# Attention and feed-forward in one kernel: maxima of keys and means of values of the third and fourth batch follow a table of steps

## The chip, the core and the metric

The kernel runs on one core of one Trainium2 chip. The core has five engines with an instruction queue each: TensorE (PE; its weight loads are shown apart as PEld), VectorE (DVE), ScalarE (ACT), GpSimd (POOL) and SyncE (SP), which here only issues transfers. Every queue is worked off in order, and an instruction that waits for a semaphore holds up all that stand behind it. Sixteen transfer engines move data between DRAM and the on-chip memory SBUF; matmul results stand in PSUM, which has eight banks. The metric is the device time of one execution in microseconds (us), lower is better.

## What is computed

Attention with a window and with summaries of blocks, and behind it a feed-forward layer, all in float32:

```python
# q, k, v: 4 batches, 8 heads, 768 positions, 64 wide; block, window = 32, 16
k_sum = k.reshape(B, H, nb, block, D).max(axis=3)
v_sum = v.reshape(B, H, nb, block, D).mean(axis=3)
scores_l = scale * np.matmul(q, k.transpose(0, 1, 3, 2))      # only where |i - j| < 16
scores_s = scale * np.einsum('bhsd,bhnd->bhsn', q, k_sum) + np.log(block)
a = softmax(concatenate([scores_l, scores_s]))
attn = a @ concatenate([v, v_sum])
x = attn as 3072 tokens x 512
h = x @ w_in                                                   # 512 x 2048
out = (h * tanh(softplus(h))) @ w_out                          # 2048 x 512
```

For each of the 24 blocks of 32 positions the attention needs the maximum of the keys, k_sum, and the mean of the values, v_sum.

## The kernel before

**Tiling.** Two heads make a pair `hp` (four pairs) and 256 positions a chunk `c` (three to a batch, twelve in all). A unit is one pair of one chunk; `todo` lists the 48 units, chunk by chunk. The fourth batch is chunks 9 to 11, units 36 to 47. The feed-forward layer works on six groups `g` of 512 tokens, in 16 columns `fc` of 128 of its 2048 middle values: 96 steps in all. A step is: products with w_in (`ph`), the activation on ScalarE, its split into a rounded part `ah` and a rest `al`, and the products with w_out (`po`) for the column two steps back. All matmuls take operands as a rounded part and a rest, three products for one.

**Stages.** Up to step 18 an order that is written out by hand places every operation. Steps 19 to 31 (about 162 to 245 us) run in a loop in which VectorE also makes sums of weight blocks (`first_sums`, `second_sums`), which go out to DRAM (`w_sums`, line 691) from a work area, the tile `results`; VectorE can write the area again only when the stores have landed. From step 32 on, two steps run together (`ff_in_pair`), with seven products of such sums and of sums of blocks of x (`x_blocks`) in place of eight. Their weights come back from DRAM in turns, 1.8 MB for each pair of steps (`load_sums`, line 725). In this part VectorE also combines the product tiles into `h` (lines 750 to 758), which frees their PSUM banks. The sums of weights end at step 40.

**Attention in the loop.** Two units start at each of the steps 19, 22, 25, 29, 33, 37, and so on by fours (`begins`): scores `sc` there, the transposes `pt_ps` two steps later, the value products `x_ps` at the next begin. Then ScalarE copies x_ps into `x_blocks`, and VectorE makes the operands of the feed-forward products from it (lines 459 to 465).

**Summaries of the blocks.** For each pair of heads of a batch a chain of four operations runs once: `load_key_source` (line 238) loads the keys `ks`, `key_summary` (line 276) takes their maxima into `km` on VectorE, `load_value_source` (line 242) loads the values `vsum`, `value_means` (lines 297 and 298) sums and scales them into `vq` on VectorE. `ks` and `vsum` of all pairs share one buffer, so each load waits until the operation before it in the chain is done. `value_summary` (line 303) then copies vq into the tile `vm`, from which `att_load_values` (line 324) fills the operand of x_ps; GpSimd copies km into the operand of the scores (`att_key_summary`, line 312). The four vm tiles of one batch are written again by the next one.

**What sets the order of these.** In `loads(i)`, called once in each step, the tables `keys` and `sums` say when `att_load_keys` (the maximum and behind it the load of values of one pair) and `att_summaries` (the means, the copy to vm and the load of keys of the next pair) run. For the third batch, with pairs 0 to 3, the maximum stands at steps 23, 25, 27 and 29 and the means one step later; for the fourth at 46, 48, 50, 52 and one step later.

Of the kernel before, what the change touches and what calls it, by code (L numbers as in the profile page):

```python
# [9 lines left out]
F32 = mybir.dt.float32  # L10
# [7 lines left out]
B, H, S, D = 4, 8, 768, 64  # L18
DM, DFF = 512, 2048
BLK, WIN = 32, 16  # L20
P = 128
NB = S // BLK
# [3 lines left out]
CH = 256  # L26
# [3 lines left out]
HP = H // 2  # L30
# [9 lines left out]
TG = CG * CH  # L40
# [29 lines left out]
def fused_kernel(ctx: ExitStack, tc: tile.TileContext, q0, qk, kt, v0, vw, vs, w_in, w_out, out):  # L70
# [3 lines left out]
    def pool(name, bufs, side):  # L74
        return ctx.enter_context(tc.tile_pool(name=name, bufs=bufs, side=side))
# [3 lines left out]
    att = pool("att", 2, "left")  # L79
    w_in_home = pool("w_in_home", 1, "left")  # L80
    maxima = pool("maxima", HP, "left")
# [142 lines left out]
        nc.gpsimd.memset(zeroed[hp][0:KW], 0.0)  # L224

    summary = {}
    xs = {}
    units = {}
    rests = {}
# [42 lines left out]
    def key_summary(b, hp):  # L272

        keys = sources.pop((b, hp, 0))
        km = maxima.tile([P, NB], F32, tag="km", name=f"km{b}_{hp}")
        nc.vector.reduce_max(km, keys.rearrange("p (n j) -> p n j", j=BLK), axis=AX.X)  # L276
        summary[b, hp] = [km]

# [35 lines left out]
    def att_load_keys(c, hp):  # L314
        b, th = divmod(c, CPB)
        if th == 0:
            key_summary(b, hp)
            load_value_source(b, hp)

    def att_load_values(c, hp):  # L320
        b = c // CPB
        vwt = att.tile([KA, NQ, P], F32, tag="vw", name=f"vw{c}_{hp}")
        nc.sync.dma_start(vwt[0:KW], vw[c, hp].rearrange("p (s k) -> p s k", s=NQ))
        nc.sync.dma_start(vwt[KW:KA], summary[b, hp][1].unsqueeze(1).broadcast_to([NB, NQ, P]))
        units[c, hp]["v"] = vwt

    def att_summaries(u):

        for i, fs in ((u, (value_means, value_summary)), (u + 1, (load_key_source,))):
            if i < len(todo) and todo[i][0] % CPB == 0:  # L330
                for f in fs:
                    f(todo[i][0] // CPB, todo[i][1])
# [325 lines left out]
    for k, word in enumerate(order):  # L658
        name, what = parse(word)
# [7 lines left out]
    dram = ctx.enter_context(tc.tile_pool(name="dram", bufs=1, space=bass.MemoryType.DRAM))  # L667
    kept = [dram.tile([P, 2, 7, CH], F32, name=f"w_sums_{p}") for p in range(NFC // 2)]
    whole_steps = WHOLE * NFC
    change = att.tile([P, CH], F32, tag="pt", name="change", bufs=1)  # L670
    area = res[0]

    def home(p):
# [87 lines left out]
    at = {}  # L761

    def put(what, i, *found):
        at.setdefault((what, i), []).extend(found)
# [4 lines left out]
    for k, i in enumerate(begins):  # L769
        pair = [2 * n + 2 + 2 * k, 2 * n + 3 + 2 * k]  # L770
        later = begins[k + 1] if k + 1 < len(begins) else i + 4
        put("scores", i, *pair)
        put("turns", i + 2, *pair)
        put("values", later, *pair)
        for j, u in enumerate(pair):
            put("norms", i + j, u)
            put("copies", i + 1 + j, u + 2)
            shift = {25: 1, 19: -1}.get(i, 0)
            put("keys", i + 1 + 2 * j + shift, u + 4)
            put("sums", i + 2 + 2 * j + shift, u + 4)  # L780

    def found(what, i):
        return [todo[u] for u in at.get((what, i), ()) if u < len(todo)]

    def loads(i):
        for u in at.get(("scores", i), ()):
            if u + 2 < len(todo):
                att_queries(*todo[u + 2])
        for unit_ in found("keys", i):
            att_load_keys(*unit_)  # L790
        for unit_ in found("copies", i):
            att_key_summary(*unit_)
        for u in at.get(("sums", i), ()):
            att_summaries(u)
        for u in at.get(("values", i), ()):
            if u + 2 < len(todo):
                att_load_values(*todo[u + 2])

    def norms(i):
        for unit_ in found("norms", i):  # L800
# [137 lines left out]
```

## Time and profile before

| | us |
|---|---|
| median of 3 runs | 651.85 |
| lowest and highest | 651.17 and 658.01 |
| the profiled execution | 656.05 |
| its span | 654.3 |
| PE busy | 610.8 (93%) |
| DVE busy | 439.7 (67%) |
| ACT busy | 339.6 (52%) |
| POOL busy | 79.6 (12%) |
| mean granted TensorE clock | 0.975 |

The profile is of one execution, and the times in it count from the start of its span. A row of the timeline gives the start and the length of an instruction, or of several alike in a row, and in brackets how long its engine stood idle before it and what released it. Matmuls are pipelined, so consecutive ones overlap. The granted clock is a share of 2.4 GHz; its lower level, 1.2 GHz, is 0.5. "DMA w_sums<-results" as a releaser means that a store to w_sums landed.

### The profile page before, as it was taken

Reading aid. Unit: us, or ns where it says so; the run is one execution under the profiler, and the core shown is the slowest. Engines: PE = TensorE matmul, PEld = TensorE weight load, DVE = VectorE, ACT = ScalarE, POOL = GpSimd, SP = SyncE. Lnnn points to the kernel's source line nnn. Section 1 sums busy time; section 2 is a strip of 40 time slices with the busy share of each in tenths; the row PEclk is TensorE's granted clock in tenths of the full one; section 3 lists DMA queues with packets and bytes.
Section 4 is the critical chain, followed back from the end, with each engine's and each line's share of the span. In section 5 each row is a group of like instructions: output and inputs, shape, how many; then the busy total and the mean of one; then the engine's idle time right before and its main releaser. Section 6 shows DMA issues by size and latency. Waiting matters only on the chain.

```text
span 654.3 us, 13016 instructions
## 1 busy us (share of the span) xinstructions
PE 610.8 (93%) x4848; PEld 527.8 (81%) x4848; DVE 439.7 (67%) x1102; ACT 339.6 (52%) x803; POOL 79.6 (12%) x119
## 2 busy tenths in 40 slices
PE   3899999999999996999499887999999999999997
PEld 3788777788888875898398776988988989898996
DVE  3999999982678585676677664664774665743433
ACT  3887668583556242753255452565566473323322
POOL 4431122110110000101011010110110110000000
PEclk9899999999999997999699988999999999999999
DMA  9978666642577865978678476776586563556411
GB/s 265 244 252 284 216 217 210 200 158 94 166 239 244 286 225 171 328 280 266 224 254 283 156 265 224 251 251 230 193 285 248 172 224 143 195 208 225 143 83 66
DMA packets 50223, 141.78 MB, mean 217 GB/s; under 512 B 8816, under 2 KB 15728, under 8 KB 50160
## 3 DMA queue, kind: packets, MB, share of 16 engines
q1 hardware_dynamic: 50160, 140.94, 64.6%
q8 instruction: 39, 0.64, 0.4%
q14 instruction: 24, 0.20, 0.1%
HBM read 117.83 MB, written 20.97 MB: 212 GB/s over the span
## 4 chain that ended last, share of the span: by engine, by line
PE 50%; DVE 20%; DMA 11%; ACT 4%; issue 3%; SPq 0%; DVEq 0%
PE po L531 24%; PE ph L740 17%; DMA w_sums<-results 6%; PE ph L503 5%; DMA vsum<-vs 4%; PE x_ps L431 2%; DVE al L521 2%; PE sc L347 1%; ACT pr L379 1%; PE pt_ps L405 1%; DVE results L699 1%; DVE vq L297 1%; DVE w L176 1%; DVE km L276 1%; DVE results L707 1%
## 5 line engine op out<-in xcount | busy, mean ns | idle before, releaser
L399 POOL TENSOR_TENSOR pr<-pr,rs 128x480 f32<-128x480 f32 x48 | 57.7, 1204 | 418.5 <-DVE rs L395 252.0
L740 PE MATMUL ph<-xh,w_early_in 128*128 128x256 f32 x512 | 99.2, 278 | 0.0
L531 PE MATMUL po<-w_early_out_hi,ah 128*128 128x512 f32 x240 | 96.2, 401 | 2.5 <-DVE results L541 2.5
L510 ACT ACTIVATE h<-h 128x512 f32<-128x512 f32 x64 | 36.9, 623 | 114.4 <-DVE h L757 114.4
L531 PE MATMUL po<-w_early_out_hi,al 128*128 128x512 f32 x240 | 94.9, 396 | 0.9 <-DVE al L521 0.9
L531 PE MATMUL po<-w_early_out_lo,ah 128*128 128x512 f32 x240 | 94.6, 394 | 0.0
L379 ACT ACTIVATE pr<-pr,nm 128x120 f32<-128x120 f32 x192 | 73.4, 384 | 24.1 <-DVE nm L368 23.9
L740 PEld LDWEIGHTS ph<-xh,w_early_in 128*128 128x128 f32 x512 | 83.4, 191 | 0.0
L521 DVE TENSOR_TENSOR al<-h,ah 128x512 fp32r<-128x512 f32 x64 | 43.1, 691 | 58.1 <-ACT ah L519 58.1
L740 PE MATMUL ph<-xl,w_early_in 128*128 128x256 f32 x256 | 71.3, 278 | 0.0
L531 PE MATMUL po<-w_late_out_hi,ah 128*128 128x512 f32 x144 | 57.1, 397 | 0.0
L531 PEld LDWEIGHTS po<-w_early_out_hi,ah 128*128 128x128 f32 x240 | 46.1, 192 | 13.1 <-DVE results L541 2.9
L531 PE MATMUL po<-w_late_out_hi,al 128*128 128x512 f32 x144 | 56.0, 389 | 0.6 <-DVE al L521 0.6
L531 PE MATMUL po<-w_late_out_lo,ah 128*128 128x512 f32 x144 | 55.9, 388 | 0.0
L531 PEld LDWEIGHTS po<-w_early_out_hi,al 128*128 128x128 f32 x240 | 45.9, 191 | 10.3 <-DVE al L521 2.0
L531 PEld LDWEIGHTS po<-w_early_out_lo,ah 128*128 128x128 f32 x240 | 45.9, 191 | 9.6
L503 PE MATMUL ph<-xh,w_early_in 128*128 128x512 f32 x160 | 52.0, 391 | 0.0
L740 PEld LDWEIGHTS ph<-xl,w_early_in 128*128 128x128 f32 x256 | 48.9, 191 | 0.0
L750 DVE TENSOR_TENSOR change<-h,ph 128x256 f32<-128x256 f32 x32 | 13.1, 410 | 50.5 <-ACT h L749 50.5
L740 PE MATMUL ph<-w_early_in 128*128 128x256 f32 x272 | 41.5, 290 | 3.3 <-DVE w_early_in L464 2.7
L740 PE MATMUL ph<-w_late_in,w_early_in 128*128 128x256 f32 x304 | 43.0, 277 | 0.5 <-DVE w_late_in L465 0.5
L746 ACT COPY h<-ph 128x512 f32<-128x512 f32 x32 | 18.8, 587 | 44.6 <-PE ph L740 44.6
(110 smaller groups left out, 1228.4 us busy)
## 6 DMA issues: line engine op xcount, KB each, us to landing
w_early_in<-w_sums SPq DMA_DIRECT2D x64, 896.0 KB
qk<-qk SPq DMA_DIRECT2D x40, 496.0 KB
w<-w_in SPq DMA_DIRECT2D x16, 512.0 KB
w<-w_out SPq DMA_DIRECT2D x16, 512.0 KB
w_sums<-results SPq DMA_DIRECT2D x32, 256.0 KB
vw<-vw SPq DMA_DIRECT2D x40, 192.0 KB
ks<-kt SPq DMA_DIRECT2D x16, 384.0 KB
out<-results SPq DMA_DIRECT2D x24, 256.0 KB
```

The source lines that it names most:

```text
L176: nc.vector.scalar_tensor_tensor(out=x, in0=high, scalar=SIGN, in1=x, op0=ALU.bitwise_and, op1=ALU.bitwise_or)
L276: nc.vector.reduce_max(km, keys.rearrange("p (n j) -> p n j", j=BLK), axis=AX.X)
L379: nc.scalar.activation(pr[:, s, :], pr[:, s, :], AF.Exp, scale=-1.0, bias=nm[:, s:s + 1], accum_out=sm[:, s:s + 1])
L399: nc.gpsimd.tensor_mul(u["p"], u["p"], u["r"].unsqueeze(2).broadcast_to([P, NQ, KA]))
L431: nc.tensor.matmul(x, u["v"][0:rows, s, d], pt, start=(c >= CG), stop=(c >= CG or s == NQ - 1))
L503: nc.tensor.matmul(turned(ph), w[:, cc * P:(cc + 1) * P], turned(x[:, cc, :]), start=(cc == 0 and n == 0), stop=(cc == NCC - 1 and n == 2))
L510: nc.scalar.activation(a, st[g, fc], AF.Mish)
L521: return lambda: nc.vector.tensor_sub(al, a, ah.bitcast(F32))
L531: nc.tensor.matmul(turned(po[g][t]), a[:, tok], turned(w), start=(fc == 0 and n == 0), stop=(fc == NFC - 1 and n == 2))
L740: nc.tensor.matmul(turned(ps[:, half * CH:(half + 1) * CH]), w_[:, a * P:(a + 1) * P], turned(x[:, a, :]), start=(a == 0 and n == 0), stop ...
L746: nc.scalar.copy(second, products(1, 3))
L750: nc.vector.tensor_sub(change, second[:, high], ps[:, low])
```

## The change

The tables `keys` and `sums` go. A new table, `chain`, gives the step of each operation by batch: it starts at step 19 for the third batch with one step from link to link, and at step 33 for the fourth with two; the value of `sent` is the step of the copy to vm. Within a pair of heads the load of keys stands at some step, the maximum and the load of values one link later, the means one link after that, together with the load of keys of the next pair. So the maxima of the third batch stand at steps 20, 22, 24 and 26, its means at 21, 23, 25 and 27; the maxima of the fourth at 35, 39, 43 and 47, its means at 37, 41, 45 and 49. Since the maxima of the fourth batch are now written while those of the third are still read, they get a place of their own, the second half of a tile (`spare`) whose first half is `change`, a work tile of VectorE.

```diff
-        km = maxima.tile([P, NB], F32, tag="km", name=f"km{b}_{hp}")
+        if b == B - 1:
+            km = maxima_home[0][:, hp * NB:(hp + 1) * NB]
+        else:
+            km = maxima.tile([P, NB], F32, tag="km", name=f"km{b}_{hp}")
...
-    change = att.tile([P, CH], F32, tag="pt", name="change", bufs=1)
+    spare = att.tile([P, TG], F32, tag="pt", name="spare", bufs=1)
+    change = spare[:, :CH]
+    maxima_home.append(spare[:, CH:])
...
-            shift = {25: 1, 19: -1}.get(i, 0)
-            put("keys", i + 1 + 2 * j + shift, u + 4)
-            put("sums", i + 2 + 2 * j + shift, u + 4)
...
+    for b, i, gap, sent in ((2, 19, 1, (22, 24, 26, 28)), (3, 33, 2, (45, 45, 49, 50))):
+        for hp in range(HP):
+            for k, f in enumerate((load_key_source, key_summary, load_value_source, value_means)):
+                chain.setdefault(i + gap * (2 * hp + (k + 1) // 2), []).append((f, b, hp))
+            chain.setdefault(sent[hp], []).append((value_summary, b, hp))
+
+    def in_order(event):
+        return (value_summary, key_summary, load_value_source, value_means, load_key_source).index(event[0])
...
-        for unit_ in found("keys", i):
-            att_load_keys(*unit_)
...
-        for u in at.get(("sums", i), ()):
-            att_summaries(u)
...
+        for f, b, hp in sorted(chain.get(i, ()), key=in_order):
+            f(b, hp)
```

Three places show what moves. In the rows, a number after a name tells the pair of heads or the column; line numbers of the change are 4 to 6 higher than those before for the same operation.

VectorE at steps 30 to 32, before (rs is the divisor of a unit, x_blocks to w_early_in make an operand, al is the rest of an activation):

```order
L394 TENSOR_SCALAR rs_1_2799<-sm_1_2734 128x4
L395 RECIPROCAL rs_1_2799<-rs_1_2799 128x4
L297 TENSOR_REDUCE vq_3_2804<-vsum_3_2754 96x32
L298 TENSOR_SCALAR vq_3_2804<-vq_3_2804 96x32
L464 CAST xh_126<-x_blocks 128x512
L465 TENSOR_TENSOR xl_127<-x_blocks,xh_126 128x512
L459 SCALAR_TENSOR_TENSOR x_blocks<-x_blocks 128x512
L464 CAST w_early_in<-x_blocks 128x512
```

The same place of the change:

```order
L398 TENSOR_SCALAR rs_1_2804<-sm_1_2743 128x4
L399 RECIPROCAL rs_1_2804<-rs_1_2804 128x4
L468 CAST xh_126<-x_blocks 128x512
L469 TENSOR_TENSOR xl_127<-x_blocks,xh_126 128x512
L463 SCALAR_TENSOR_TENSOR x_blocks<-x_blocks 128x512
```

The means of the last pair of the third batch have left the place between the divisor and the operand; they stand three steps earlier.

SyncE at steps 37 to 40, before (w_early_in<-w_sums are weight sums that come back, w_sums<- are their stores):

```order
L324 DMA vw_1_3325<-vm_1_2532 24x4x128
L725 DMA w_early_in<-w_sums_1969 128x1792 x2
L691 DMA w_sums_1970<-w_late_in 128x512 x2
L691 DMA w_sums_1970<-results 128x512 x4
L691 DMA w_sums_1970<-results 128x256 x2
L725 DMA w_early_in<-w_sums_1970 128x1792 x2
L691 DMA w_sums_1971<-w_late_in 128x512 x2
```

The same place of the change:

```order
L328 DMA vw_1_3330<-vm_1_2361 24x4x128
L239 DMA ks_1_3336<-kt 128x768
L731 DMA w_early_in<-w_sums_1969 128x1792 x2
L697 DMA w_sums_1970<-w_late_in 128x512 x2
L697 DMA w_sums_1970<-results 128x512 x4
L697 DMA w_sums_1970<-results 128x256 x2
L243 DMA vsum_1_3464<-vs 96x1024
L731 DMA w_early_in<-w_sums_1970 128x1792 x2
L697 DMA w_sums_1971<-w_late_in 128x512 x2
```

A load of keys and a load of values of the fourth batch have come in, one ahead of the weight sums and their stores, one behind the stores.

VectorE at steps 46 and 47 (pair 48 of steps follows with the sums h), before:

```order
L465 TENSOR_TENSOR w_late_in<-x_blocks,w_late_in 128x512
L276 TENSOR_REDUCE km_0_4023<-ks_0_3918 128x24
L521 TENSOR_TENSOR al_15_4041<-h_15_3945,ah_15_4040 128x512
L297 TENSOR_REDUCE vq_0_4045<-vsum_0_4025 96x32
L298 TENSOR_SCALAR vq_0_4045<-vq_0_4045 96x32
L750 TENSOR_TENSOR change<-h_1_4078,ph_0_1_4093 128x256
```

The same place of the change:

```order
L469 TENSOR_TENSOR w_late_in<-x_blocks,w_late_in 128x512
L525 TENSOR_TENSOR al_15_4065<-h_15_3973,ah_15_4064 128x512
L280 TENSOR_REDUCE spare<-ks_3_3952 128x24
L756 TENSOR_TENSOR spare<-h_1_4098,ph_0_1_4113 128x256
L757 TENSOR_TENSOR spare<-h_1_4098,spare 128x256
```

Where the first pair of heads had its maximum and its means, one directly after the other, the last pair has its maximum now.

## Rows read from the trace of the kernel before

**Rows 1.** By stretch: length, busy PE, PEld, DVE, ACT, POOL, clock, DMA share, GB/s.

```profile
203.00:228.00 25.00, 25.00 (x178) 20.70 (x176) 17.49 (x46) 12.23 (x30) 2.39 (x4) 1.00 0.85 271
...
240.60:263.20 22.60, 15.27 (x77) 13.02 (x75) 14.70 (x33) 9.40 (x24) 2.50 (x4) 0.85 0.64 206
...
263.00:311.00 48.00, 48.00 (x414) 42.95 (x414) 33.48 (x90) 25.79 (x64) 5.44 (x8) 1.00 0.86 291
...
370.00:430.00 60.00, 52.30 (x410) 45.44 (x408) 36.93 (x101) 28.58 (x71) 5.17 (x8) 0.91 0.70 237
```

**Rows 2.** Chain that ended last, pieces of x_ps: start us, us, what.

```profile
263.25 1.08 PE x_ps L431 x32
...
346.17 1.11 PE x_ps L431 x32
...
430.30 1.08 PE x_ps L431 x32
...
453.87 1.11 PE x_ps L431 x32
...
478.10 1.08 PE x_ps L431 x32
```

**Rows 3.** Timeline of VectorE and TensorE, late stretch: start, length, instruction, [idle before].

```profile
382.85 1.22 DVE L297 TENSOR_REDUCE vq<-vsum 96x32 f32<-96x1024 f32 x1 [2.62 <-DMA vsum<-vs]
...
385.99 0.60 PE L531 MATMUL po<-w_early_out_hi,ah 128*128 128x512 f32 x1 [2.52 <-DVE results L541]
...
401.82 1.22 DVE L297 TENSOR_REDUCE vq<-vsum 96x32 f32<-96x1024 f32 x1 [7.83 <-DMA vsum<-vs]
...
404.75 0.63 PE L347 MATMUL sc<-qk 64*64 64x120 f32 x2 [3.35 <-DVE h L752]
```

**Rows 4.** Timeline of SyncE and VectorE, late stretch: loads of vsum, a use.

```profile
366.31 0.34 SPq L242 DMA_DIRECT2D vsum<-vs  x1
...
369.51 1.22 DVE L297 TENSOR_REDUCE vq<-vsum 96x32 f32<-96x1024 f32 x1 [2.63 <-DMA vsum<-vs]
...
393.42 0.33 SPq L242 DMA_DIRECT2D vsum<-vs  x1
```

**Rows 5.** Timeline of VectorE and TensorE, early stretch.

```profile
231.24 1.23 DVE L707 TENSOR_TENSOR results<-w_early_in 128x1024 f32<-128x1024 f32 x1 [8.43 <-DMA w_sums<-results]
...
241.74 0.92 DVE L276 TENSOR_REDUCE km<-ks 128x24 f32<-128x768 f32 x1
...
248.62 0.65 PE L405 MATMUL pt_ps<-ident,pr 128*120 128x128 f32 x4 [3.81 <-POOL pr L399]
...
252.59 1.22 DVE L297 TENSOR_REDUCE vq<-vsum 96x32 f32<-96x1024 f32 x1 [5.19 <-DMA vsum<-vs]
...
256.29 0.35 PE L740 MATMUL ph<-w_early_in 128*128 128x256 f32 x1 [2.66 <-DVE w_early_in L464]
```

**Rows 6.** Timeline of VectorE and TensorE, between the two stretches.

```profile
310.33 0.69 DVE L713 TENSOR_TENSOR results<-results 128x512 f32<-128x512 f32 x1 [4.80 <-DMA w_sums<-results]
...
320.12 0.63 PE L347 MATMUL sc<-qk 64*64 64x120 f32 x2 [8.10 <-DMA w_early_in<-w_sums]
...
325.65 0.69 DVE L713 TENSOR_TENSOR results<-results 128x512 f32<-128x512 f32 x1 [1.98 <-DMA w_sums<-results]
...
329.89 0.96 PE L740 MATMUL ph<-w_early_in 128*128 128x256 f32 x6 [0.32 <-DVE nm L368]
```

**Rows 7.** Timeline of VectorE, GpSimd and TensorE, steps 22 to 27.

```profile
185.49 0.28 DVE L368 CUSTOM_DVE_ANT_0 pr<-sc,base 128x120 f32<-128x120 f32 x1 [1.31 <-PE sc L347]
...
215.94 0.99 POOL L399 TENSOR_TENSOR pr<-pr,rs 128x480 f32<-128x480 f32 x1 [5.85 <-PE ph L503]
...
218.44 1.04 PE L405 MATMUL pt_ps<-ident,pr 128*120 128x128 f32 x8
```

**Rows 8.** Transfers by line: queue, operation, count, KB each.

```profile
vsum<-vs SPq DMA_DIRECT2D x12, 384.0 KB
```

**Rows 9.** Waits of SyncE's queue: what waited, for what, us, times, longest.

```profile
SPq L242 <- DVE km L276: 11.4, 4, 8.6
```

More of the change, by code (lines that the diff above doesn't have):

```diff
@@ L226, in fused_kernel @@
     summary = {}
+    maxima_home = []
     xs = {}
@@ L777, in fused_kernel @@
             put("copies", i + 1 + j, u + 2)
-            shift = {25: 1, 19: -1}.get(i, 0)
-            put("keys", i + 1 + 2 * j + shift, u + 4)
-            put("sums", i + 2 + 2 * j + shift, u + 4)
     def found(what, i):
         return [todo[u] for u in at.get((what, i), ()) if u < len(todo)]
+    chain = {}
+    for b, i, gap, sent in ((2, 19, 1, (22, 24, 26, 28)), (3, 33, 2, (45, 45, 49, 50))):
[5 more added lines that the diff above has]
+        return (value_summary, key_summary, load_value_source, value_means, load_key_source).index(event[0])
     def loads(i):
```

## The prediction

> **What bounds the kernel now.** I read the busy times first: TensorE works in 93% of the span, so what can be won is where it stands still or runs at a low clock. The views by stretch name two such places that hold the moved work [rows 1]: from 240.6 to 263.2 us TensorE is busy 15.27 of 22.60 us at a mean granted clock of 0.85, and from 370 to 430 us 52.30 of 60.00 us at 0.91. Then the chain of work that ended last, whose x_ps pieces (the value product of two units, line 431) mark equal portions of work [rows 2]. In undisturbed work two of them are 453.87 - 430.30 = 23.57 us apart. From 346.17 to 430.30 lie three such portions, in 84.13 us instead of 70.7: 13.4 us are lost there. From 263.25 to 346.17 lie three too, in 82.92 us: 12.2 us lost.
>
> **What ends each loss.** In the late stretch it is the wait for values that were loaded just before their use [rows 3]: VectorE stands at the sum of vsum (line 297) for 2.62 us before 382.85 and 7.83 us before 401.82. Behind it in VectorE's order wait the copies of results and the sums h, which free PSUM banks, and TensorE waits for those, 2.52 us before 385.99 and 3.35 us before 404.75. The reason stands in SyncE's own order: the load issued at 393.42 was used at 401.82, 8.4 us later, the one issued at 366.31 at 369.51, 3.2 us [rows 4]; VectorE ran out of other work in between.
>
> In the early stretch two things add up [rows 5]. VectorE waited 8.43 us, until 231.24, for stores of weight sums to land, and ran late from there. It reached the maximum of keys at 241.74 (0.92 us), while TensorE stood 3.81 us before 248.62 for a normalized unit. Then it waited 5.19 us for vsum and summed it at 252.59 (1.22 us), and only then made the block that TensorE waited for, 2.66 us before 256.29.
>
> Between them lies a third loss that the change doesn't name [rows 6]. VectorE waits until 310.33 and 325.65 (4.80 and 1.98 us) for stores of weight sums, the sums h come late, and TensorE stands 8.10 us before 320.12 and 0.32 us before 329.89. The transfer engines are busy 0.86 of the 48 us before 311, at 291 GB/s [rows 1].
>
> **The change, part by part.** The same 8 maxima, 8 means and 16 loads remain, plus a place for four tiles of maxima; TensorE's and ScalarE's orders don't change. So nothing is removed but waits, and each moved instruction must find room where it goes.
>
> *Fourth batch, late stretch.* The eight waits with load and use in one or two steps become two full steps, about 11.8 us (half of 23.57), against 3.2 to 8.4 us from issue to use above. The three sums and maxima left there (at steps 45, 47, 49) have their data. I take 13.4 us less the 0.7 us that a portion with copies of results loses anyway (478.10 - 453.87 = 24.23 against 23.57 [rows 2]): **-12.7 us**. Bounds: 13.4 if nothing remains, 5.9 if only the two waits shown on TensorE go (2.52 + 3.35) and nothing of the clock comes back.
>
> *Third batch, early stretch.* The maximum at 241.74 goes: 0.92 us less of the 3.81. The wait of 5.19 and the sum of 1.22 go: the 2.66 us vanish, because the block is then ready 6.4 us sooner. The clock: 0.85 on average over 22.60 us is 2 x 0.15 x 22.6 = 6.8 us at the lower of its two levels (1.2 against 2.4 GHz), after waits, which costs up to 3.4 us; half of it, 1.7, belongs to the second wait. Together **-5.3 us**. The wait of 8.43 stays: those stores lie behind the same loads of weight sums in both orders. Bounds: 0.9 (only the maximum counts) and all 7.33 us of idle time with 3.4 of clock, 10.7.
>
> *Third batch, where it goes (steps 19 to 27, about 160 to 220 us).* TensorE doesn't wait there now: it is busy 25.00 of the 25.00 us from 203 [rows 1]. VectorE has gaps (1.31 us before 185.49), and the last slack is at 218.44, where transposes start 1.5 us after the normalization at 215.94 ended (0.99 us long) [rows 7]. Eight operations of 0.92 and 1.22 us come three steps earlier, but eight of the same kind leave those steps three later, so only the first three steps carry more. New waits come with a lead of one step: a sum of values waits for a load that SyncE could issue only after the maximum before it. I estimate from the 3.2 us of a free queue and the lead of one step (at most a quarter of 23.57, 5.9) that VectorE gets up to 3 us later by step 26, of which 1.5 are covered: **+1.3 us**. Bounds: 0 and 3.
>
> *Fourth batch, where it goes (steps 33 to 43, the third loss).* Five loads of 384 KB [rows 8] join the queue before the stores on which VectorE waits. One takes 393216 B / 291 GB/s = 1.35 us. Two lie right ahead of the stores that land before 310.33, and one ahead of those before 325.65: 2.7 + 1.35, on TensorE's path because its waits of 8.10 and 0.32 end with that chain. The maxima and sums moved to these steps run beside the same waits, but for the sum at step 41 (1.22 us, half of it covered, an estimate): 0.6. Together **+4.6 us**. Bounds: 0, if 14% of idle transfer time in the 48 us (6.7 us) takes all five, and 8.0, five loads of 1.35 and one sum of 1.22.
>
> The Trainium skill, page "DMA: Bandwidth & Descriptors", section "Queues, rings and completion order", says that each transfer engine consumes descriptors in ring order. By that rule alone every load that is moved ahead of a store delays it, 5 x 1.35 = 6.75 us instead of 4.05, and the time would be 2.7 us more. The idle share of 0.14 says that the ring runs empty in between, so I count three. It is the rule that speaks most against this change.
>
> *The four maxima in the spare half of the tile for "change"*: waits of VectorE on the other half are the same as before, in its order, so nothing.
>
> **Sum.** -12.7 - 5.3 + 1.3 + 4.6 = -12.1 us. The profiled execution took 656.05 us (span 654.3 and 1.75 around it), which gives 643.95. The median of the three runs shown is 651.85, 4.2 lower than that execution, and the same subtraction from it gives **639.7 us**.
>
> **Rivals.**
> *All of it goes.* VectorE, freed of four operations and a wait, catches up before 231 us too, and idle transfer time takes the added loads: -12.7 - 10.7 = -23.4, 628.4 us. For it: the 14% idle time; against it: the 8.43 us wait hangs on loads that are not moved.
>
> *The third loss swallows it.* Both bounds of cost, +3 and +8.0, and only 2.5 us of the early stretch: -12.7 - 2.5 + 11.0 = -4.2, 647.6 us, within the 1% that a measurement of this kernel can tell from no change. For it: three losses in a row where VectorE waits for stores; against it: TensorE comes to that stretch earlier by what it saves, and the transfers with it.
>
> *The waits stay.* The loads of vsum wait for the maximum before them (SyncE stood 11.4 us for that in 4 waits, at most 8.6 [rows 9]), so they may be issued so late that half of the late loss remains: -6.3 - 5.3 + 5.9 = -5.7, 646.1 us.
>
> *Slower.* SyncE issues in order: a chain load that waits for VectorE holds up the stores behind it, and VectorE waits for those stores, so both wait in a circle. Place: steps 20 to 26 and 35 to 41, eight loads with stores behind. Price: the mean wait of such a load, 11.4 / 4 = 2.85 us, eight times, 22.8: -18.0 + 5.9 + 22.8 = +10.7, 662.6 us. It gets slower by over 1% from 2.3 us each ((18.0 - 5.9 + 6.5) / 8). Against it: in the order of the change the maximum stands ahead of the weight sums whose stores come next, so the load waits no longer than those stores do anyway.
>
> **How the numbers follow.** Forecast 0.55 (its own range 634 to 645), all of it 0.12, swallowed 0.20, waits stay 0.06, slower 0.07. Faster by over 1% is below 645.3 us: the forecast but for a few hundredths, the first rival and some of the second, 0.75; within 1% 0.18; slower 0.07. The range runs from the first rival to a little over the second: 628 to 649 us.
>
> **What would show it.** No wait of VectorE's sum of values for vsum over 1 us; x_ps pieces in the late stretch 23.6 to 24.3 us apart; in the early one a single wait near 3 us before the second transposes and none for the block; the wait of 8.43 still there within 1 us or so; the wait of 8.10 us grown to 10 to 11 us. I am wrong if the late stretch still loses over 3 us, if TensorE waits before 230 us for over 3 us, or if the third loss shrinks.

## The result and the profile after

The kernel after takes 647.41 us (median of 15 runs), the kernel before, run beside it, 654.28 (15 runs): a ratio of 0.9904 with an interval of 0.9876 to 0.9932. It is faster by 6 to 7 us, a little over half of the 12.1 that were forecast; the interval is clear of no change, but leaves open whether the gain is above or below 1%. The forecast of 639.7 us was too low; the time lies inside the range of 628 to 649. The profiled execution took 649.86 us, with a span of 648.1.

The first view is by stretch, cut at the x_ps pieces of steps 29, 33, 45, 49 and 57 (columns as in [rows 1]).

```profile
205.00:235.80 30.80, 27.71 (x168) 22.48 (x162) 19.61 (x50) 11.99 (x29) 2.86 (x4) 0.89 0.83 274
235.80:261.60 25.80, 24.62 (x189) 21.00 (x188) 20.93 (x52) 13.43 (x32) 3.16 (x4) 1.00 0.63 200
261.60:345.70 84.10, 75.34 (x615) 66.73 (x615) 62.44 (x161) 40.38 (x102) 7.83 (x12) 0.94 0.86 289
345.70:376.80 31.10, 26.27 (x207) 23.04 (x208) 19.72 (x52) 13.09 (x34) 2.59 (x4) 0.95 0.57 199
376.80:423.90 47.10, 47.10 (x411) 42.23 (x410) 28.67 (x85) 28.71 (x70) 5.44 (x8) 1.00 0.72 247
```

The late stretch is cured from step 49 on: TensorE works in all 47.10 us at full clock. But two places lose that lost nothing before: the portion before 235.80, where TensorE was always busy [rows 1], and the one from 345.70 to 376.80, 31.1 us where the kernel before needs 24.2. The chain that ended last (start, length, what) says what stands in the second.

```profile
345.72 1.08 PE x_ps L435 x32
...
348.97 6.98 DMA vw<-vm
356.01 1.95 DMA vm<-vq
357.98 1.23 DVE vq L301
...
376.81 1.08 PE x_ps L435 x32
...
400.38 1.08 PE x_ps L435 x32
...
423.94 1.08 PE x_ps L435 x32
```

The timeline of the same place, SyncE's issues first, then VectorE, TensorE and ScalarE:

```profile
342.92 0.80 SPq L731 DMA_DIRECT2D w_early_in<-w_sums  x2
347.46 0.81 SPq L311 DMA_DIRECT2D qk<-qk  x2
350.51 0.82 SPq L328 DMA_DIRECT2D vw<-vm  x1
356.01 1.68 SPq L307 DMA_DIRECT2D vm<-vq  x2
...
357.98 1.22 DVE L301 TENSOR_REDUCE vq<-vsum 96x32 f32<-96x1024 f32 x1 [6.08 <-DMA vm<-vq]
...
365.32 0.62 PE L409 MATMUL pt_ps<-ident,pr 128*120 128x128 f32 x4 [3.82 <-DVE h L758]
...
366.59 1.15 ACT L514 ACTIVATE h<-h 128x512 f32<-128x512 f32 x2 [10.68 <-DVE h L763]
```

The sum of values at step 45 had its values; they were issued at 341.80. It waited 6.08 us for the buffer of its result. The tag vq has two buffers, and the sum's buffer held the first mean of the batch, which the table copies out only at step 45 too. SyncE issued that copy at 356.01, after standing still since 351.3, because the copy overwrites a vm that the transfers vw<-vm ahead of it still read. These landed late. An estimate of why: ahead of them in the queue lay two loads of weight sums of 896 KB each, two of queries of 496 KB and two of values of 192 KB (sizes from the page's list of transfers), 3.24 MB, and at 291 GB/s [rows 1] that is 11.1 us from 342.92, about 354. Behind the sum stood everything that TensorE needs from VectorE: block, normalization and sums h.

The early stretch, by VectorE, TensorE and SyncE:

```profile
195.30 0.79 SPq L307 DMA_DIRECT2D vm<-vq  x1
196.20 0.45 SPq L243 DMA_DIRECT2D vsum<-vs  x1
...
200.17 1.22 DVE L301 TENSOR_REDUCE vq<-vsum 96x32 f32<-96x1024 f32 x1 [2.42 <-DMA vsum<-vs]
...
209.46 0.69 DVE L719 TENSOR_TENSOR results<-results 128x512 f32<-128x512 f32 x1 [2.55 <-DMA w_sums<-results]
...
224.22 1.11 PE L409 MATMUL pt_ps<-ident,pr 128*120 128x128 f32 x4 [3.09 <-POOL pr L403]
...
236.39 1.23 DVE L713 TENSOR_TENSOR results<-w_early_in 128x1024 f32<-128x1024 f32 x1 [7.35 <-DMA w_sums<-results]
...
253.37 0.65 PE L409 MATMUL pt_ps<-ident,pr 128*120 128x128 f32 x4 [1.18 <-POOL pr L403]
```

Here too a copy of a mean stood ahead of a load (195.30 and 196.20), so the second sum waited 2.42 us; VectorE waited another 2.55 us for a store, and TensorE stood 3.09 us before 224.22 at the transposes that had been in time before [rows 7]. Behind that wait the granted clock was 0.74 up to the next x_ps piece, and this same work took 11.59 us; in a kernel below with the same order here (e2_third_only), after a wait of 1.24 us, the clock was 1.00 and it took 8.75 us (after first, then e2; columns as above).

```profile
224.22:235.81 11.59, 11.59 (x41) 9.22 (x41) 4.68 (x9) 1.80 (x3) 0.83 (x2) 0.74 0.90 304
```

```profile
218.92:227.67 8.75, 8.75 (x41) 7.07 (x41) 4.79 (x9) 1.81 (x3) 0.36 (x2) 1.00 0.91 296
```

So nearly half of the 6.2 us that this portion lost is clock. Then, from step 29 to 33, the waits of 3.81 and 2.66 us [rows 5] are down to one of 1.18. The third loss between the stretches is as it was [rows 6]:

```profile
309.50 0.69 DVE L719 TENSOR_TENSOR results<-results 128x512 f32<-128x512 f32 x1 [4.87 <-DMA w_sums<-results]
...
319.28 0.63 PE L351 MATMUL sc<-qk 64*64 64x120 f32 x2 [8.17 <-DVE h L758]
...
324.94 0.69 DVE L719 TENSOR_TENSOR results<-results 128x512 f32<-128x512 f32 x1 [2.11 <-DMA w_sums<-results]
```

This table lists every kernel that was run. The pieces are distances in us between the x_ps pieces of the steps named, from the starts of their first matmuls in the timeline of one profiled execution each (the chain gives each start up to 0.07 us later). Each ratio is to runs of the kernel before made beside that kernel; their medians lie between 652.39 and 654.28.

| kernel | median, us | ratio to before (interval) | 25-29 | 29-33 | 22-33 | 33-45 | 45-49 | 49-57 |
|---|---|---|---|---|---|---|---|---|
| before | 654.28 | 1 | 24.9 | 35.6 | 80.0 | 82.9 | 24.2 | 59.9 |
| after | 647.41 | 0.9904 (0.9876-0.9932) | 31.1 | 25.8 | 76.3 | 84.1 | 31.1 | 47.1 |
| e1_means_apart | 641.33 | 0.9798 (0.9764-0.9833) | 31.0 | 25.9 | 76.4 | 83.6 | 24.9 | 47.1 |
| e2_third_only | 650.03 | 0.9931 (0.9900-0.9961) | 26.4 | 29.9 | 75.8 | 81.7 | 24.2 | 60.4 |
| e3_fourth_only | 649.10 | 0.9933 (0.9904-0.9961) | 24.9 | 34.4 | 78.8 | 83.4 | 31.3 | 47.1 |
| e4_third_from_20 | 643.16 | 0.9832 (0.9797-0.9868) | 24.9 | 27.5 | 71.9 | 83.8 | 30.6 | 47.1 |
| e5_both | 638.30 | 0.9788 (0.9753-0.9823) | 24.9 | 30.0 | 74.3 | 83.0 | 24.9 | 47.1 |
| e6_load_first | 639.49 | 0.9798 (0.9761-0.9835) | 25.1 | 29.9 | 74.4 | 83.0 | 24.9 | 47.1 |
| e7_mean_later | 642.36 | 0.9840 (0.9801-0.9878) | 29.7 | 29.0 | 78.2 | 84.4 | 24.2 | 48.7 |
| e8_third_from_21 | 636.39 | 0.9757 (0.9724-0.9790) | 24.9 | 28.5 | 72.9 | 83.0 | 24.9 | 47.1 |
| e9_stores_first_early | 635.56 | 0.9749 (0.9714-0.9784) | 24.9 | 28.7 | 73.1 | 84.0 | 24.9 | 47.1 |
| e10_stores_first_late | 632.78 | 0.9693 (0.9659-0.9727) | 24.9 | 29.6 | 73.9 | 79.9 | 24.9 | 47.1 |
| e11_stores_first | 633.43 | 0.9714 (0.9683-0.9745) | 24.9 | 29.3 | 73.7 | 79.9 | 24.9 | 47.1 |
| e12_loads_after_sums | 630.43 | 0.9655 (0.9625-0.9686) | 24.9 | 26.5 | 70.9 | 80.3 | 24.9 | 47.1 |

After against before by these pieces: -3.7 us from step 22 to 33, +1.2 from 33 to 45, +6.9 from 45 to 49, -12.8 from 49 to 57, in sum -8.4. One execution scatters by more than a microsecond: the third batch is issued alike in before and e3, which show 80.0 and 78.8 us from step 22 to 33, and alike in after, e1, e2 and e7, which show 75.8 to 78.2. The two profiled spans differ by 6.2 only, since the execution of after that was profiled had lost 2.1 us by step 22, where the kernels are nearly the same (the first moved operations stand at steps 19 to 21); its clock in the first 40 us was 0.87, against 0.96 in that of before.

### The profile page after: what moved, and what is told of

Same layout as the page of the kernel before. It is cut to its first block, busy times and chain, and to the rows that moved or that the text cites. A ratio compares the mean times of both kernels' runs of the same rounds, so it can differ in the third digit from the quotient of the medians.

```text
span 648.1 us, 13016 instructions
## 1 busy us (share of the span) xinstructions
PE 610.4 (94%) x4848; PEld 527.1 (81%) x4848; DVE 438.6 (68%) x1102; ACT 340.2 (52%) x803; POOL 79.7 (12%) x119
## 4 chain that ended last, share of the span: by engine, by line
PE 57%; DVE 23%; DMA 9%; ACT 4%; issue 4%; SPq 1%; POOL 1%; DVEq 0%; POOLq 0%; ACTq 0%
PE po L535 27%; PE ph L746 19%; PE ph L507 5%; DMA w_sums<-results 5%; PE x_ps L435 2%; PE sc L351 2%; DVE al L525 2%; DVE pr L372 2%; PE pt_ps L409 2%; DMA vw<-vm 2%; DVE w L176 1%; DVE results L705 1%; DVE w_f L185 1%; ACT pr L383 1%; DVE w L172 1%
## 5 line engine op out<-in xcount | busy, mean ns | idle before, releaser
L756 DVE TENSOR_TENSOR spare<-h,ph 128x256 f32<-128x256 f32 x32 | 13.1, 410 | 55.2 <-ACT h L755 55.1
L746 PEld LDWEIGHTS ph<-w_late_in,w_early_in 128*128 128x128 f32 x304 | 39.8, 191 | 3.0 <-DVE w_late_in L469 1.0
```

The lines of the kernel that those rows point to most:

```text
L746: nc.tensor.matmul(turned(ps[:, half * CH:(half + 1) * CH]), w_[:, a * P:(a + 1) * P], turned(x[:, a, :]), start=(a == 0 and n == 0), stop ...
L756: nc.vector.tensor_sub(change, second[:, high], ps[:, low])
```

## The experiments

Each edit is made to the kernel after unless another is named. These theories led the experiments. The gain of the late stretch came in full, and 6.9 us of it were lost again to one wait for a buffer (theory A). The early stretch gained what was forecast in sum, by a gain and a stall that belong together (theory C: the stall before step 29 comes from the wait for the second vsum; theory E: stores that land late, behind large loads, set the piece of step 33 and make the third loss).

**e1_means_apart.** The means of the fourth batch get homes of their own, beside the maxima:

```diff
-        vq = means[b, hp] = att.tile([VP, BLK], F32, tag="vq", name=f"vq{b}_{hp}")
+        if b == B - 1:
+            vq = means[b, hp] = maxima_home[0][0:VP, HP * NB + hp * BLK:HP * NB + (hp + 1) * BLK]
+        else:
+            vq = means[b, hp] = att.tile([VP, BLK], F32, tag="vq", name=f"vq{b}_{hp}")
```

> The kernel after, except that the four tiles of means of the fourth batch lie in the spare half of the tile beside the four maxima, instead of in a tag of two buffers. The order of all engines stays; only the wait of the sum at step 45 (and 49) for the copy of an older mean out of its buffer falls away. Theory A (the sum at step 45 waited 6.08 us for that copy, which SyncE issued at 356.01 behind transfers, and this alone made the new loss of 6.9 us between the x_ps pieces at 345.72 and 376.81): no wait of VectorE there, these pieces 23.6 to 24.3 us apart, 6.9 us less than the kernel after, ratio to before about 0.980. Rival B (SyncE itself, which issues nothing from 351.3 to 356.0 us, is what holds the stretch up): the wait moves to a load, and the time stays within 2 us of the kernel after, ratio 0.987 to 0.993.

The order of the built program shows the one wait that goes, after above, e1 below:

```
674 L301 TENSOR_REDUCE vq_2_3949<-vsum_2_3770 96x32 [waits DMAHW7_49,DMAHW0_49]
674 L304 TENSOR_REDUCE spare<-vsum_2_3768 96x32 [waits DMAHW7_49]
```

Measured: 641.33 us, 0.9798, which is 0.0106 less than the kernel after, or 6.9 us. In the timeline of e1 (its lines from 301 on stand three higher) the sum follows the reciprocal with no idle time ahead of it, while SyncE still issues the copies only at 355.06:

```profile
350.30 0.18 DVE L402 RECIPROCAL rs<-rs 128x4 f32<-128x4 f32 x1
350.39 1.18 DVE L304 TENSOR_REDUCE spare<-vsum 96x32 f32<-96x1024 f32 x1
...
355.06 1.68 SPq L310 DMA_DIRECT2D vm<-spare  x2
```

The pieces of steps 45 and 49 stand 24.9 us apart instead of 31.1, a little over the 24.3 that were expected at most. SyncE stands still as long as before (349.82 to 355.06 us, against 351.33 to 356.01) and costs nothing now, so rival B is out: the stall was the wait for the buffer.

**e2_third_only and e3_fourth_only.** One batch by the table; for the other the lines that the change removed are back, and in e2 the fourth batch's maxima have their old tag again (the table's row is shown):

```diff
-    for b, i, gap, sent in ((2, 19, 1, (22, 24, 26, 28)), (3, 33, 2, (45, 45, 49, 50))):
+    for b, i, gap, sent in ((2, 19, 1, (22, 24, 26, 28)),):       (e2; e3 keeps only the row of batch 3)
```

> Only the third batch follows the table, the fourth is issued as in the kernel before. From the traces: the steps 25 to 29 take 6.15 us longer than before, the steps 29 to 33 9.84 us less, so the part brings -3.7 us, ratio about 0.994. The forecast on record had -5.3 + 1.3 = -4.0 for it, ratio 0.994 too, but with a stall of at most 1.5 us in the steps 25 to 27. Rival: the two stretches are independent of the batch moved, and the early one gains nothing or loses: ratio 1.00 or above.

> Only the fourth batch follows the table, the third is issued as in the kernel before. From the traces: -12.9 us in the steps 49 to 57, +6.9 us in the steps 45 to 49 (the wait of 6.08 us at the sum of step 45), +1.2 us in the steps 37 to 45: -4.8 us, ratio about 0.993. The forecast on record had -12.7 + 4.6 = -8.1 us, ratio 0.988, with the third loss grown by 4.6 us and nothing lost at step 45. If the +1.2 us comes from the five loads moved there, the pieces at steps 33, 37, 41 and 45 stand 1.2 us further apart in sum than before also here; if it is chance of an execution, they don't.

Measured: 0.9931 and 0.9933, as expected from the traces. Together they would make 1 - 0.0069 - 0.0067 = 0.9864; the whole change has 0.9904, and with 0.003 to either side of each of the three that is within what can be told. In e3 the pieces of steps 45 and 49 stand 31.3 us apart: the stall belongs to the fourth batch alone. From step 33 to 45 they stand 83.4 apart, 0.5 us more than before, which is too little to tell whether the 1.2 us of after come from the moved loads or from chance. In e2's profile the third batch behaves nearly as the forecast had it: +1.5 us from step 25 to 29 and -5.7 from 29 to 33, with these rows.

```profile
218.92 0.65 PE L410 MATMUL pt_ps<-ident,pr 128*120 128x128 f32 x4 [1.24 <-POOL pr L404]
...
231.10 1.23 DVE L714 TENSOR_TENSOR results<-w_early_in 128x1024 f32<-128x1024 f32 x1 [7.15 <-DMA w_sums<-results]
...
248.10 1.11 PE L410 MATMUL pt_ps<-ident,pr 128*120 128x128 f32 x4 [3.36 <-POOL pr L404]
```

VectorE's and ScalarE's orders in these steps are the same as in the kernel after, which shows +6.2 and -9.8. The split differs from execution to execution, with the clock: from its wait for stores to the piece of step 33, e2 ran at 0.94 and after at 1.00. The sum differs less: -4.2 from step 22 to 33 here, -3.7 in after, -3.6 in e1, but -1.8 in e7, which has this order too.

**e4_third_from_20 and e8_third_from_21.** The third batch's row of the table one step later on the kernel after, and two steps later on e1:

```diff
-    for b, i, gap, sent in ((2, 19, 1, (22, 24, 26, 28)), (3, 33, 2, (45, 45, 49, 50))):
+    for b, i, gap, sent in ((2, 20, 1, (23, 25, 27, 29)), (3, 33, 2, (45, 45, 49, 50))):       (e8: 2, 21, 1, (24, 26, 28, 30))
```

> The kernel after, with the third batch's row of the table one step later (keys loaded at steps 20, 22, 24, 26, means at 22, 24, 26, 28, copies of means at 23, 25, 27, 29). Theory C: the stall of 6.15 us in the steps 25 to 29 of the kernel after comes from VectorE's lateness, in which the wait of 2.42 us for the second vsum before 200.17 us weighs most; SyncE issued that load at 196.20, behind the copy of a mean, which stood behind the transfers of the values of step 22. One step later load and copy fall on other steps, the wait shrinks, and half or more of the stall goes, 3 to 5 us less than the kernel after, ratio 0.983 to 0.986; the steps 29 to 33 keep their gain within 2 us. Rival D: the stall comes from the number of maxima and sums in steps 21 to 26 alone, and four of them are still there: less than 2 us less than the kernel after, ratio 0.988 to 0.992.

> The kernel e1_means_apart with the third batch's row of the table two steps later (keys loaded at steps 21, 23, 25, 27, means at 23, 25, 27, 29, copies of means at 24, 26, 28, 30): one step ahead of the kernel before, where e4_third_from_20 is two and the kernel after three ahead. Between the x_ps pieces of steps 22 and 33 lie 80.0 us in the kernel before, 71.9 in e4_third_from_20, 76.3 in the kernel after and in e1_means_apart. If the place among the weight sums decides (maxima on steps 22, 24, 26, 28 beside the second sums as in the kernel after, on odd steps in e4), this one is at 75 to 78 us, ratio 0.978 to 0.984. If the lead alone decides, with two steps as the best, it lies between e4 and the kernel before, 74 to 78 too; then the stall before step 29 is gone (25 to 29 at 25 us) and the loss sits in the steps 29 to 33. So the place of the loss tells them apart.

Measured: 0.9832, as theory C had it, and 0.9757, below what either answer for e8 expected. In both the stall before step 29 is gone (24.9 us), and the pieces of steps 29 and 33 keep most of their gain. For e8 the answers had expected 75 to 78 and 74 to 78 us from step 22 to 33; 72.9 is under either, with the loss in the steps 29 to 33, as the second answer placed it. e8 differs from e1 by the row alone and has 0.0041 less in the ratio, some 2.7 us, with intervals that overlap: a lead of one step is no worse than one of three, and probably better.

**e5_both.** e1 and e4 in one kernel.

> Both edits that gained, in one kernel: the fourth batch's means in the spare half of the tile, and the third batch's row of the table one step later. If the two stalls have nothing to do with each other, their gains on the kernel after (641.33 and 643.16 us against 647.41) add up: -6.1 - 4.2 us, about 637 us, ratio 0.971 to 0.976. Rival: TensorE's earlier arrival lets a third wait take half of the second gain back, ratio 0.977 or above.

Measured: 638.30 us, 0.9788. By the ratios the two gains did not add up; the interval just reaches the upper end of what the sum would be, so that they do is not excluded. In the profile the stall of steps 45 to 49 is gone as in e1, but the steps 29 to 33 take 30.0 us, against 27.5 in e4, with the same order of instructions: TensorE waited 3.34 us there and its next four transposes took 1.11 us, in e4 it waited 2.90 and they took 0.66. The granted clock from step 29 to 33 was 0.94 here and 1.00 in e4. So the 2.5 us by which these steps differ go with the clock of one execution, and how much e4's edit is worth stays uncertain by about that.

**e6_load_first.** On e1, in the third batch the load of values goes out ahead of the copy of an older mean:

```diff
+        if event[1] == 2:
+            return (key_summary, load_value_source, value_summary, value_means, load_key_source).index(event[0])
         return (value_summary, key_summary, load_value_source, value_means, load_key_source).index(event[0])
```

> The kernel e1_means_apart (fourth batch's means apart, ratio 0.980), with one thing changed in the third batch: in a step that has both, SyncE issues the load of values ahead of the copy of the older mean. Theory C (the wait of 2.26 us for the second vsum comes from that copy, which held SyncE until 195.30 us in the kernel after): that wait goes, the pieces at steps 25 and 29 stand 2 to 5 us closer than the 31.0 us there, the piece at step 33 comes 2 to 4 us earlier, ratio 0.974 to 0.977. Rival D (the number of operations, or stores that land late, make the stall): the wait goes, the pieces don't move by more than 1 us, ratio 0.978 to 0.982.

Measured: 0.9798, the same ratio as e1. The rows of e6 (no idle time ahead of the second sum now):

```profile
194.23 1.18 DVE L304 TENSOR_REDUCE vq<-vsum 96x32 f32<-96x1024 f32 x1
...
229.77 1.22 DVE L716 TENSOR_TENSOR results<-w_early_in 128x1024 f32<-128x1024 f32 x1 [7.32 <-DMA w_sums<-results]
...
246.76 1.11 PE L412 MATMUL pt_ps<-ident,pr 128*120 128x128 f32 x4 [3.35 <-POOL pr L406]
```

Theory C fits the cause of the stall: without the wait, the pieces of steps 25 and 29 stand 25.1 us apart, and 24.9 in all kernels whose table row starts later; with it they stand 31.1, 31.0, 29.7 and 26.4 apart (after, e1, e7, e2), after waits of 2.42, 2.26, 2.14 and 1.48 us at the second sum. It fails for what this is worth. The steps 29 to 33 take 29.9 us instead of 25.9, so the piece of step 33 comes only 1.9 us sooner, and the ratio, as rival D had it, shows nothing (it could hide the 1.9). The steps wait for the landing of stores (7.32 us here), which comes 47.9 us after the piece of step 22, 51.2 in e1: 6 us of stall less brought it forward by 3.3. In the nine kernels that move the third batch and leave the early loads of weight sums where they were (after, e1, e2, e4 to e8, e10), the piece of step 33 comes 25.2 to 27.4 us after that landing: 25.2 or 25.3 where the clock was 1.00 in between (after, e1, e4), 26.5 to 27.4 where it was 0.94. So a stall ahead of the landing is in part time in which TensorE would have stood later, and the rest of the 4.0 us that e6 lost again (1.3 us behind the landing) goes with the lower clock.

**e7_mean_later.** The tag keeps its two buffers; the sum of the fourth batch's third unit, and the load of keys that takes its place, go one step back:

```diff
+                held = (f, b, hp) in ((value_means, 3, 2), (load_key_source, 3, 3))
-                chain.setdefault(i + gap * (2 * hp + (k + 1) // 2), []).append((f, b, hp))
+                chain.setdefault(i + gap * (2 * hp + (k + 1) // 2) + held, []).append((f, b, hp))
```

> The kernel after, with the means still in a tag of two buffers, but the sum of the fourth batch's third unit (and the load of keys behind it, which takes the same place) at step 46 instead of 45. Theory A (the buffer's copy is late by 6 us): by then the buffer is free, the sum waits less than 1 us; the maximum at step 47 then stands close behind the load of its keys and waits 1 to 3 us. The pieces at steps 45 and 49 stand 25 to 27.5 us apart instead of 31.1: 3.5 to 6 us less than the kernel after, ratio 0.981 to 0.985. If not the buffer but the load of keys, late at 359.23 us, or the row of transfers itself decides, the pieces stay 30 us or more apart, ratio 0.988 to 0.992.

```profile
363.92 1.21 DVE L301 TENSOR_REDUCE vq<-vsum 96x32 f32<-96x1024 f32 x1
...
368.06 0.95 DVE L280 TENSOR_REDUCE spare<-ks 128x24 f32<-128x768 f32 x1 [2.13 <-DMA ks<-kt]
```

Measured: 642.36 us, 0.9840. The wait for the buffer is gone without a byte more of room, the maximum waits 2.13 us as expected, and the pieces stand 24.2 us apart, less than expected; 1.5 us come back in the next portion (49 to 57: 48.7). By the pieces 5.4 of the 6.9 us are won, by the ratios 4.2.

**e9, e10, e11 and e12: what holds the rest.** On e8, the loads of weight sums (two of 896 KB each time) change places with the stores on which VectorE waits:

```diff
         send()
         loads(i)
+        if whole_steps - i in (5, 3):                       (e9, e11; e12: in (3, 2))
+            load_sums((5 - whole_steps + i) // 2)           (e12: load_sums(3 - whole_steps + i))
...
-        if whole_steps - i in (6, 4):                       (e9, e11, e12)
-            load_sums(3 - (whole_steps - i) // 2)           (e9, e11, e12)
...
         ff_in_pair(*steps[i], pair, lambda: second_exponents(i))
-        load_sums(pair + 2)                                 (e10, e11, e12)
...
         send()
+        load_sums(pair + 2)                                 (e10, e11, e12)
         loads(i)
```

> The kernel e8_third_from_21 (ratio 0.976), with the two early loads of weight sums (w_early_in from w_sums, 1.84 MB each) moved from the end of steps 26 and 28 to steps 27 and 29, behind the stores of the weight sums made one step before. Theory E (these stores, issued behind 1.84 MB of loads, end VectorE's wait of 5.89 us before 228.20 us, 8.43 us in the kernel before, and that moment sets the piece at step 33 in every variant): the wait shrinks to 3 us or less, the pieces at steps 29 and 33 stand 24 to 25.5 us apart instead of 28.5, 3 to 4 us less, ratio 0.969 to 0.973. Rival F (transfers as a whole are the limit there, whatever their order): the wait moves to the next stores or to the loads, pieces within 1 us, ratio 0.974 to 0.978.

> The kernel e8_third_from_21, with the loads of weight sums of the paired steps (from step 32 on) issued behind the stores of the step before them instead of ahead. Theory E for the third loss (VectorE waits 3.19 us before 301.74 and 2.72 us before 317.78 for stores that lie behind 1.84 MB of loads; TensorE waits 6.48 us before 311.52 at the end of that chain): both waits shrink below 1 us, TensorE's to 3 us or less, the pieces at steps 41 and 45 stand 27 to 31 us apart instead of 34.6, 4 to 7 us less, ratio 0.965 to 0.970. Rival F (the sum of the transfers is the limit): the wait moves to the loads of weight sums themselves, which now come later, pieces within 1.5 us, ratio 0.973 to 0.978.

> Both moves of the loads of weight sums behind the stores. If the two losses are independent, the gains add: 7 to 11 us less than e8_third_from_21, ratio 0.959 to 0.966. Rival: TensorE comes to the third loss earlier by what the early stretch gives, the transfers do not, and the second gain shrinks by as much: ratio 0.966 to 0.971.

> The kernel e10_stores_first_late (ratio 0.969), with the two early loads of weight sums issued in steps 29 and 30, behind all stores on which VectorE waits in steps 27 and 28 (in e9_stores_first_early, one step later than before, the wait only passed on to the next stores: 6.21 us before 231.73). Theory E (each load of 1.84 MB ahead of stores on which VectorE waits costs its transfer of some 6 us, wherever it stands among them): with none there, VectorE's waits for stores in steps 27 and 28 stay at 2 us or less, no wait of TensorE over 1 us before the piece at step 33, pieces at steps 29 and 33 24 to 25.5 us apart instead of 29.6, 4 us less, ratio 0.962 to 0.966. Rival G (the loads then come too late for the pair at step 32, or hold up the queries and values of step 33): a wait of TensorE for w_early_in or VectorE for the loads, pieces 28 us or more apart, ratio 0.968 or above.

Measured: 0.9749, 0.9693, 0.9714 and 0.9655. One step later (e9) the early loads delay the next stores instead, as rival F had it; the first wait goes from 5.89 us in e8 to 0.64 and the second grows to 6.21:

```profile
220.92 1.23 DVE L716 TENSOR_TENSOR results<-w_early_in 128x1024 f32<-128x1024 f32 x1 [0.64 <-DMA w_sums<-results]
...
231.73 0.69 DVE L722 TENSOR_TENSOR results<-results 128x512 f32<-128x512 f32 x1 [6.21 <-DMA w_sums<-results]
```

Behind all of them (e12) no wait for stores over 1.53 us is left in steps 22 to 28, TensorE waits once, for the loads that now come late (part of rival G), and the piece of step 33 comes 3.1 us sooner than in e10, with 26.5 us from step 29 where 24 to 25.5 were expected:

```profile
228.83 0.69 DVE L722 TENSOR_TENSOR results<-results 128x512 f32<-128x512 f32 x1 [0.88 <-DMA w_sums<-results]
...
245.97 1.48 PE L749 MATMUL ph<-w_early_in 128*128 128x256 f32 x10 [1.72 <-DMA w_early_in<-w_sums]
```

In the third loss (e10) VectorE's waits of 3.19 and 2.72 us at the second sums are gone, while one at a first sum grew from 0.80 to 2.73; TensorE's wait fell from 6.48 us in e8 to 5.13, and the steps 33 to 45 take 79.9 us instead of 83.0 (31.5 from step 41 to 45, a little over the 31 expected at most):

```profile
306.47 1.22 DVE L716 TENSOR_TENSOR results<-w_late_in 128x1024 f32<-128x1024 f32 x1 [2.73 <-DMA w_sums<-results]
...
311.11 0.63 PE L354 MATMUL sc<-qk 64*64 64x120 f32 x2 [5.13 <-DVE h L761]
```

The ratio came as theory E had it, the wait less: five of the 6.5 us stay, and what holds them was not tested. In e11 the gains did not add up: 0.9714 is above the range of the answer and even of its rival (0.966 to 0.971), and e11 and e10 cannot be told apart. e12's ratio lies below e8's with intervals that do not touch, so for the two moves together the gain is shown (6.7 us by the ratios). e12, at 630.43 us, is the fastest of all, some 16 us below the kernel after by the ratios; what it adds to the change is the means apart, the third batch's row two steps later, and loads behind stores.

## Where the prediction held and where it failed

- **Late stretch, -12.7 us:** right, -12.8 from step 49 to 57 in the profile of after, and 23.6 us from piece to piece.
- **The step that failed:** "The three sums and maxima left there (at steps 45, 47, 49) have their data." They had. But the sum at step 45 also needs its result's buffer, whose copy the table sets at the same step, behind transfers. I had counted the reads of each moved instruction and not what it overwrites. The sum waited 6.08 us for that copy, and the portion lost 6.9 us, of which e1 gives back 6.2 (24.9 us instead of 31.1; 6.9 by the ratios). The order of the change shows it without a run, as a second semaphore at that sum.
- **Fourth batch in the third loss, +4.6:** too large. After shows +1.2 us, and the waits of 8.10, 4.80 and 1.98 us [rows 6] became 8.17, 4.87 and 2.11 instead of growing. Over the nine kernels with the table's fourth batch and the loads of weight sums in their old places there (after, e1, e3 to e9), steps 33 to 45 take 83.6 us on average, 83.0 to 84.4 one by one, against 82.9 and 81.7 in the two without (before, e2): the term is about 1.3 us, with an uncertainty as large. The count of five loads, in the bound of 8.0 and in the 6.75, was one too many: four go out ahead of the last stores on which VectorE waits (at 268.01, 281.27, 295.68 and 313.87 us in after; the fifth, at 332.70, follows these stores). That idle transfer time took most of the four fits the numbers; no run tests it by itself. The Trainium skill ("DMA: Bandwidth & Descriptors", section "Queues, rings and completion order") says that descriptors are consumed in ring order; the price of 6.75 us that I worked out from it did not come for these loads of 384 KB. Where 1.84 MB lie ahead of stores on which an engine waits, e9, e10 and e12 agree with it: the wait follows the place of the loads.
- **Third batch, -5.3 + 1.3 = -4.0:** near in sum (-3.7 in after, -4.2 in e2, but -1.8 in e7; -2.7 as the mean of the four kernels with this order against the two without), by luck in part, for both terms were too small in after: +6.2 and -9.8. The +1.3 is no result of its own sentence either (3 less 1.5 is 1.5). In after's profile the normalization that the transposes of step 27 follow started at 223.18 us against 215.94 [rows 7]; without the 2.1 us from the start of the program that is 5 us late, not 3, and 1.5 of it were covered. TensorE stood 3.09 us there, one of the signs named for being wrong, and the clock behind the wait, which the term had put at nothing, cost nearly as much again. The second sum waited 2.42 us for vsum, where I had written that none would wait over 1. Much of what was lost there was won again from step 29 to 33, because the landing of the stores sets that end. I had named that wait (8.43 us, 7.35 after) and that it would stay, but added up gain and loss as if they were independent.
- **The sum:** -12.8 - 3.7 + 1.2 + 6.9 = -8.4 by pieces, against -12.1. Of the 7.7 us between 639.7 and 647.4, 3.7 are these pieces and 2.4 come from the base: I subtracted from the median of the three runs shown, 651.85, where 15 runs give 654.28. The other 1.5 or so lie between the pieces of one execution (-8.4) and the medians (-6.9) and stay open.
- **The rivals:** the time of "The third loss swallows it", 647.6, is nearly the one measured, but by luck: it is 4.2 us under a base that was 2.4 too low, and its mechanism did not come, since that loss grew by 1.2 us. A wait did take the place of the one removed, on a buffer that no rival named. SyncE's order did hold VectorE up through copies, not in the circle of "Slower" and for one large wait, not eight.

## What to carry to other kernels

When an instruction is moved earlier, list what it waits for on both sides: its inputs, and the last reader of the buffer that it overwrites, with the step and the queue from which that reader goes out. A stall ahead of a moment that something else helps to set (here the landing of stores) is not to be summed with what follows, and removing it gains only as far as that moment moves: in e6 a stall of 6 us went, the landing came 3.3 us sooner and the next piece 1.9. In this kernel, large loads of data not yet due belonged behind the smaller stores that VectorE waited for: moving them there (e8 to e12) took the ratio from 0.9757 to 0.9655.

## What the runs showed of the hardware

The same instructions at the start of the program ran at different clocks from one execution to the next. From after and from e2, the first 40 us:

```profile
0.00:40.00 40.00, 27.21 (x471) 23.14 (x472) 26.68 (x112) 24.46 (x90) 16.57 (x41) 0.87 0.95 272
```

```profile
0.00:40.00 40.00, 27.03 (x510) 23.26 (x511) 29.17 (x118) 28.01 (x100) 19.22 (x45) 1.00 0.98 281
```

The piece of step 22 came at 185.28 us in the one and at 181.83 in the other, 3.5 us apart, half of what the change is worth. That the clock made all of it is not shown; pieces counted from step 22 leave it out. A wait's length alone did not tell either whether TensorE ran on at half clock: four transposes took 1.11 us after waits of 3.09 us (after) and 2.49 (e8), and 0.65 after one of 3.81 [rows 5]. And a small transfer took long with large ones ahead of it: vw<-vm (48 KB), issued at 348.97 in after behind the loads of weight sums, queries and values named above, released the next copy 6.98 us later.
